# Seven stretches of zero matmuls on TensorE in the last quarter of a fused attention and rational-activation kernel

## Chip, cores and metric

The kernel runs on one core of a Trainium2 chip. The metric is the device time of one execution in microseconds (us), as the median of several runs. Beside it stands one profiled execution, whose trace gives the start, the duration and the reason for waiting of every instruction.

## What is computed

The reference is a polynomial-sketch linear attention followed by a two-layer network whose activation is a rational function. For 4 batches, 4 heads, 1088 positions and head size 32, with sketches S1 and S2 of rank 8:

```
phi(x)[i,j] = (S1 x)[i] * (S2 x)[j]            # 64 features per head
kv = sum_s phi(k) v^T ;  z = sum_s phi(k)
x  = (phi(q) kv) / (phi(q) z + 1e-6)           # 4352 tokens x 128
h  = x @ w_in                                  # 128 -> 2048
P  = a0 + a1 h + a2 h^2 + a3 h^3
Q  = 1 + |b0| |h| + |b1| h^2
out = (P / (Q + 1e-6)) @ w_out                 # 2048 -> 128
```

All inputs and the output are float32; the activation and the second layer are done in bfloat16.

## The kernel before

The tokens are split into chunks of 512 (the first into two of 256), and a last chunk of 256 gathers the 64 positions left over from each of the four batches. For each chunk the attention part makes `xT` (128 x tokens). The network part then goes through the 2048 hidden units in groups, numbered g0 to g22. A group of a full chunk is 8 blocks of 128 hidden units by 512 tokens, that is 4096 elements on each partition; the groups of the last chunk, g19 to g22, have 2048, 1024, 512 and 512. Each group takes these steps:

- TensorE multiplies `w_in` by `xT` into the PSUM buffer `h_ps` (line 793), and ScalarE copies it to `hb` in bfloat16 (line 799).
- VectorE makes |h|, the quadratic and the cubic by multiplications and scalings (lines 819 to 843 and 913 to 924); some sums are done by DMAs that add, issued by GpSimd (line 896).
- ScalarE makes 1/Q as exp(-ln Q): line 832 is the logarithm into `L`, line 836 the exponential into `u`.
- VectorE multiplies `y` by `u` (line 828).
- TensorE multiplies by the scaled `w_out` and adds up in the PSUM buffer `out_ps` (line 856, 8 matmuls of 512 columns for a full group; line 851 for the last chunk, by token). There are two forms: groups of terms "2" and "2d" have one such step with `u` and one with `y`, groups of terms "s" and "t" only the one with `y`. These steps are called "pr" (from u) and "py" (from y) here: py 16 is the one of g16.
- After the last group of a chunk ScalarE copies `out_ps` to `o_sb` (line 861), TensorE transposes that (line 866), ScalarE copies the transposes to `oT` (line 871) and SyncE stores it. The last chunk needs no transposes (line 981).

Buffers set much of the order: `out_ps` exists once, so the first product of the next chunk waits until ScalarE has copied it; `y` and `u` exist three times, so the first VectorE step that writes a new `y` (line 840 or 924) waits until the py step of three groups earlier has read its buffer. `kv_ps`, one PSUM bank, holds the key sums of a batch; the last batch's sums have been read before the stretches that matter here.

All steps are recorded with `plan.add(engine, ns, function, after=..., take=..., give=...)`, and `ORDER`, a fixed list of step numbers at the top of the file, says in which sequence they are issued. Each engine runs its own instructions strictly in that sequence. A new step takes the next free number and stands where `ORDER` names it.

The kernel already has matmuls whose result nobody reads: `warm` (line 352) multiplies a 128x128 by a 128x512 block of bfloat16 zeros, both read from one zero per partition. Eight of them stand at the very start and two in the first chunk, written to `out_ps`:

```python
def warm(n):
    for _ in range(n):
        nc.tensor.matmul(warm_ps[0], lhsT=zero.broadcast_to([128, 128]), rhs=zero.broadcast_to([128, CW]),
                         start=True, stop=True)
```

Of the kernel before, what the change touches and what calls it, by code (L numbers as in the profile page):

```python
# [12 lines left out]
FP = mybir.dt.float32  # L13
# [31 lines left out]
    566, 274, 275, 604, 603, 287, 277, 288, 622, 624, 627, 605, 610, 606, 586, 625, 567, 568, 626, 628, 642, 276,  # L45
    611, 523, 278, 644, 643, 612, 587, 607, 613, 289, 646, 279, 614, 645, 648, 635, 647, 280, 668, 290, 629, 569,
    649, 608, 669, 636, 637, 630, 670, 593, 291, 594, 631, 671, 638, 609, 651, 292, 293, 650, 652, 657, 653, 674,
    672, 294, 673, 689, 658, 659, 675, 615, 660, 616, 295, 632, 691, 676, 639, 431, 690, 692, 570, 693, 617, 682,
    571, 633, 695, 654, 634, 694, 661, 683, 618, 677, 684, 678, 572, 696, 717, 640, 655, 641, 698, 685, 656, 699,
    704, 697, 705, 715, 662, 716, 679, 706, 663, 718, 700, 686, 707, 732, 725, 746, 680, 687, 701, 664, 719, 726,  # L50
    733, 702, 681, 720, 703, 688, 619, 740, 760, 734, 741, 721, 727, 747, 735, 665, 722, 708, 736, 728, 723, 709,
    748, 710, 742, 749, 750, 711, 737, 743, 754, 729, 730, 755, 756, 724, 738, 666, 744, 731, 620, 739, 757, 761,
    667, 751, 762, 745, 768, 752, 763, 753, 712, 764, 769, 524, 765, 766, 525, 770, 713, 758, 759, 771, 714, 772,
    767, 773, 774, 775]


class Plan:
# [66 lines left out]
def kernel(  # L124
# [13 lines left out]
    nc = tc.nc  # L138
    B, H, S, D = q.shape
# [9 lines left out]
    CW = JC * 128  # L149
# [9 lines left out]
    WARM = (0, 0)  # L159
    GAPS = {}  # L160
    XWARM = (2, 0)
    ZEROS = 8
    USED = set(TERMS.values())
    ADDED = [i for i, kinds in ((1, "d1"), (0, "1")) if any(k in t for t in USED for k in kinds)]
# [15 lines left out]
    kvps = ctx.enter_context(tc.tile_pool(name="kvps", bufs=1, space=PSUM))  # L180
# [4 lines left out]
    plan = Plan(BUFS)  # L185
    T = {}

    def tile_of(pool, name, shape, dtype):
        return pool.tile(shape, dtype, name=name, bufs=BUFS[name])
# [110 lines left out]
    for b in range(2, B):  # L300
        for i, (name, go) in enumerate(mains(b)):
            ld[name, b] = load("SP", go, 1024 if name == "v" else 512, rank=-70 + i,
                               take=["v_aug" if name == "v" else "kq"])
# [3 lines left out]
    zero = nc.const_aps.tensor(0.0, (128, 1), FP).bitcast(BF)[:, 0:1]  # L307
# [42 lines left out]
# [5 lines that stand above are left out]
    def first_warm():  # L355
        warm_ps.append(ops.tile([128, CW], FP, name="out_ps", bufs=1))
        warm(ZEROS)

    c_zero = plan.add("DVE", 250, lambda: nc.vector.memset(zeros, 0.0), rank=-99)
    c_mask = plan.add("POOL", 1350, pool_mask, rank=-99.5)  # L360
    c_pool = plan.add("POOL", 1950, pool_consts, after=[c_mask], rank=-99)
    c_warm = plan.add("PE", 430 * ZEROS, first_warm, after=[], rank=-99, take=["out_ps"])

# [216 lines left out]
    def lab(n):  # L580
        return n - 1 if n > 1 else ("0", "0b")[n]

    def add_queries(n, nt, srcs, weights, kv_lhs, load_steps, kv_steps, w_steps, rank, give=(), early=False,
# [116 lines left out]
        def x_transposes(t):  # L700
            T["xTp", n, t] = tile_of(aps, "w_ps", [128, CW], FP)
            for i in range(2):
                nc.tensor.transpose(T["xTp", n, t][:, i * 128:(i + 1) * 128],
                                    in_=T["x", n][:, 2 * t + i].rearrange("p h d -> p (h d)"), identity=ident)
            warm(XWARM[n])

# [10 lines left out]
        def rest(s):  # L717
# [13 lines left out]
            else:  # L731
                dv = xe = xt = None
                nds = {}
                for t in range(nt // 2):
                    for hp in range(NP):
# [8 lines left out]
                                  take=["o_sb"] if t == 0 else [], give=["w_ps"], name=f"div {lab(n)},{t}")  # L744
                    s = plan.add("PE", 110 * 2 + 216 * XWARM[n], lambda t=t: x_transposes(t), after=[dv, xt], rank=rank + 0.05, take=["w_ps"],
                                 give=["o_sb"] if t == nt // 2 - 1 else [], name=f"x tr {lab(n)},{t}")
# [279 lines left out]
    for n in range(len(chunks) + 1):  # L1026

        rank = first_of[n] - 2.6
# [34 lines left out]
    for g, G in enumerate(groups):  # L1063
        G["x_step"] = x_steps[G["n"]]
        G["prev_o"] = o_step
        o_step = add_group(g, G)
    plan.issue()


# [28 lines left out]
```

## Time and profile before

| | |
|---|---|
| median of 3 runs | 266.84 us (266.09 to 266.88) |
| the profiled execution's own time | 266.53 us |
| its span, first to last instruction | 264.8 us, so 1.7 us lie around it |
| TensorE matmul | 236.0 us busy, 89% |
| VectorE | 243.2 us busy, 92% |
| ScalarE | 238.7 us busy, 90% |
| mean granted TensorE clock | 0.971 |

PE is TensorE's matmuls, PEld its weight loads, DVE VectorE, ACT ScalarE, POOL GpSimd. A number in square brackets on a line is the idle time of that engine just before it, with what ended it. PEclk is the share of TensorE's clock that was granted.

### The profile page before, as it was taken

What the parts mean: (1) busy time and instruction counts of PE and PEld (TensorE: products, weight loads), DVE (VectorE), ACT (ScalarE), POOL (GpSimd) and SP (SyncE); (2) the same over time, 40 slices, a digit from 0 to 9 for tenths busy, and PEclk for the clock granted to TensorE, in tenths of its full rate; (3) what the DMA queues carried; (4) which work ended last, traced back from release to release, by engine and by line L of the source; (5) the groups of instructions that cost most, each with busy time, mean ns of one, the idle gap of its engine ahead of it and who ended that gap; (6) DMA issues with size and microseconds to landing.
All of it is one profiled execution on the core that took longest, in us unless ns stands there. A gap on an engine that the chain in (4) does not pass through costs nothing.

```text
span 264.8 us, 3028 instructions
## 1 busy us (share of the span) xinstructions
PE 236.0 (89%) x1115; PEld 140.5 (53%) x1126; DVE 243.2 (92%) x240; ACT 238.7 (90%) x211; POOL 42.8 (16%) x63
## 2 busy tenths in 40 slices
PE   7999999999999999989899998999999788296561
PEld 4889897755656654434464545544434335153251
DVE  1658999989999999999999999999999999999882
ACT  3249798889989999999999999999999999999883
POOL 4800010101211112011201121101221111111000
PEclk9999999999999999999999999999999999769598
DMA  6987929953789996848798879954799978698512
GB/s 173 300 229 154 163 82 180 219 80 62 176 158 107 170 192 85 103 79 150 136 131 149 155 94 189 188 104 87 131 156 109 187 163 101 79 184 136 96 40 102
DMA packets 36607, 36.94 MB, mean 139 GB/s; under 512 B 18160, under 2 KB 30448, under 8 KB 36464
## 3 DMA queue, kind: packets, MB, share of 16 engines
q0 software_dynamic: 11664, 25.69, 62.2%
q1 hardware_dynamic: 24496, 10.95, 15.8%
q8 instruction: 9, 0.15, 0.2%
q10 hardware_dynamic: 432, 0.10, 0.2%
q14 instruction: 6, 0.05, 0.1%
HBM read 8.82 MB, written 2.23 MB: 42 GB/s over the span
## 4 chain that ended last, share of the span: by engine, by line
PE 44%; ACT 25%; DVE 21%; issue 8%; DVEq 0%; ACTq 0%
PE h_ps L793 20%; DVE y L828 9%; ACT L L832 7%; ACT hb L799 7%; ACT u L836 6%; PE out_ps L856 6%; PE kv_ps L488 6%; ACT u L808 3%; PE w_ps L452 2%; PE w_ps L606 2%; PE w_ps L653 2%; DVE u L828 2%; DVE y L840 2%; PE w_ps L666 2%; PE w_ps L442 2%
## 5 line engine op out<-in xcount | busy, mean ns | idle before, releaser
L793 PE MATMUL h_ps<-xT,w_in_sb 128*128 128x512 f32 (+1 forms) x320 | 126.6, 533 | 0.9 <-ACT hb L799 0.9
L793 PEld LDWEIGHTS h_ps<-xT,w_in_sb 128*128 128x128 f32 x320 | 57.6, 191 | 43.5 <-issue 34.5
L799 ACT CAST hb<-h_ps 128x1024 bf16<-128x1024 f32 (+1 forms) x70 | 70.8, 1036 | 5.7 <-PE h_ps L793 5.4
L836 ACT ACTIVATE u<-L 128x4096 bf16<-128x4096 f32 (+3 forms) x23 | 63.6, 2766 | 0.3
L828 DVE TENSOR_TENSOR y<-y,hb 128x4096 bf16<-128x4096 bf16 (+3 forms) x37 | 58.7, 1593 | 0.1
L832 ACT ACTIVATE L<-u,one_ap 128x4096 f32<-128x4096 bf16 (+3 forms) x17 | 43.4, 2553 | 0.5 <-DVE u L828 0.5
L828 DVE TENSOR_TENSOR y<-y,u 128x4096 bf16<-128x4096 bf16 (+3 forms) x23 | 39.8, 1729 | 0.2
L856 PEld LDWEIGHTS <-w_out 128*128 128x128 bf16 x208 | 20.9, 102 | 36.0 <-issue 21.8
L856 PE MATMUL out_ps<-y,w_out 128*128 128x512 bf16 (+1 forms) x136 | 33.4, 381 | 7.3 <-DVE y L828 6.8
L896 POOL DMA_DIRECT2D u<-lin x9 | 10.9, 1207 | 104.3 <-ACT ab L460 25.7
L832 ACT ACTIVATE L<-u,one_ap,b_rel 128x4096 f32<-128x4096 bf16 x6 | 23.2, 3872 | 0.0
L913 DVE TENSOR_TENSOR lin<-hb 128x4096 bf16<-128x4096 bf16 x9 | 20.6, 2286 | 0.0
L896 POOL DMA_DIRECT2D y<-lin x9 | 12.0, 1333 | 49.7 <-DVE y L828 15.7
L828 DVE TENSOR_TENSOR u<-lin,u 128x4096 bf16<-128x4096 bf16 (+3 forms) x14 | 19.2, 1373 | 0.2
L819 DVE TENSOR_SCALAR u<-hb 128x4096 int16<-128x4096 int16 (+3 forms) x20 | 18.5, 924 | 0.7 <-ACT hb L799 0.5
L896 POOL DMA_DIRECT2D y<-zeros x7 | 11.9, 1695 | 41.6 <-DVE y L828 23.2
L856 PE MATMUL out_ps<-u,w_out 128*128 128x512 bf16 (+1 forms) x62 | 13.6, 352 | 2.6 <-ACT u L836 2.4
L488 PEld LDWEIGHTS kv_ps<-v_aug,k_p 128*128 128x128 f32 x128 | 15.3, 192 | 1.1 <-DVE y L828 0.2
L488 PE MATMUL kv_ps<-v_aug,k_p 128*128 128x66 f32 x128 | 15.8, 273 | 0.0
L840 DVE TENSOR_SCALAR y<-hb,a_sb 128x4096 bf16<-128x4096 bf16 (+3 forms) x14 | 12.7, 910 | 1.5 <-PE out_ps L856 1.5
L660 ACT COPY q_pT<-w_ps 128x512 f32<-128x512 f32 (+1 forms) x20 | 10.5, 551 | 2.6 <-PE w_ps L653 2.6
L824 DVE TENSOR_SCALAR lin<-u,b_abs 128x4096 bf16<-128x4096 bf16 (+3 forms) x14 | 12.3, 877 | 0.0
(100 smaller groups left out, 255.6 us busy)
## 6 DMA issues: line engine op xcount, KB each, us to landing
u<-lin POOLq DMA_DIRECT2D x9, 1024.0 KB, 7.9
y<-lin POOLq DMA_DIRECT2D x9, 1024.0 KB, 8.3
y<-zeros POOLq DMA_DIRECT2D x6, 1024.0 KB, 11.0
out_dram<-oT SPq DMA_DIRECT2D x7, 256.0 KB, 3.7
kq<-in_k_dram SPq DMA_DIRECT2D x3, 512.0 KB, 5.3
v_aug<-in_v_dram SPq DMA_DIRECT2D x12, 128.0 KB, 5.3
kq<-in_q_dram SPq DMA_DIRECT2D x3, 512.0 KB, 4.3
w_in_sb<-in_moe_w_in_dram SPq DMA_DIRECT2D x1, 1024.0 KB, 5.4
```

What stands on the lines that cost most here:

```text
L488: nc.tensor.matmul(T["kv", b][:, hp * 66:(hp + 1) * 66], lhsT=lhs(hp), rhs=rhs(hp), start=(first and hp == 0), stop=final, skip_group_chec ...
L793: nc.tensor.matmul(T["h", g, s][:, i * W:(i + 1) * W], lhsT=w_in_sb[:, fi * 128:(fi + 1) * 128], rhs=T["xT", n][:, :W], start=True, stop=True)
L799: nc.scalar.copy(out=T["hb", g][:, s * W:(s + nsub) * W], in_=T["h", g, s][:, :nsub * W])
L819: nc.vector.tensor_scalar(out=u().bitcast(mybir.dt.int16), in0=hb().bitcast(mybir.dt.int16), scalar1=0x7FFF, scalar2=None, op0=AX.bitwise_and)
L824: nc.vector.tensor_scalar(out=lin(), in0=u(), scalar1=b_abs[:, 1:2], scalar2=b_abs[:, 0:1], op0=AX.mult, op1=AX.add)
L828: return lambda: nc.vector.tensor_mul(out=out(), in0=in0(), in1=in1())
L832: nc.scalar.activation(out=T["L", g, l0][:, :lw], in_=T["u", g][:, l0:l0 + lw], func=ACT.Ln, bias=one_ap, scale=b_rel[:, 0:1] if terms == ...
L836: nc.scalar.activation(out=T["u", g][:, l0:l0 + lw], in_=T["L", g, l0][:, :lw], func=ACT.Exp, scale=-1.0)
L840: nc.vector.tensor_scalar(out=y(), in0=hb(), scalar1=a_sb[:, 3:4], scalar2=a_sb[:, 2:3], op0=AX.mult, op1=AX.add)
L856: nc.tensor.matmul(T["o", n][:, :W], lhsT=W_terms[w][:, fis[i], :], rhs=T[src, g][:, i * W:(i + 1) * W], start=(start and i == 0), stop=(s ...
L896: nc.gpsimd.dma_start(out=dst(), in_=src(), accum_op=AX.add, max_dma_last_dim=4096)
L913: nc.vector.tensor_mul(out=sq(), in0=hb(), in1=hb())
```

## The change

Seven new steps on TensorE, numbered 776 to 782 and called hot 0 to hot 6, issue 2, 6, 23, 4, 18, 4 and 3 zero matmuls, 60 in all, of the same kind as `warm`. They write the `kv_ps` buffer, after the last batch's key sums were read from it, and nobody reads what they write. The order of all other steps stays, on TensorE and on every other engine. In TensorE's own sequence they stand here:

| step | zero matmuls | TensorE's instruction before it | and after it |
|---|---|---|---|
| hot 0 | 2 | h (L793) | the x products of the last chunk (L666, 64 columns) |
| hot 1 | 6 | h (L793) | pr 15 (L856 from u) |
| hot 2 | 23 | h (L793, 256 columns) | py 16 (L856 from y) |
| hot 3 | 4 | h (L793, 256 columns) | pr 17 (L856 from u) |
| hot 4 | 18 | h (L793, 256 columns) | the transposes of the chunk of g15 and g16 (L866) |
| hot 5 | 4 | these transposes | py 18 (L856 from y) |
| hot 6 | 3 | py 18 | pr 19 (L851 from u) |

Line numbers below the list HOT grow by one. The diff, with the lines of ORDER cut to the places where a number is new:

```diff
...
-    672, 294, 673, 689, ...
-    571, 633, 695, 654, 634, ...
...
+    672, 776, 294, 673, 689, ...
+    682, 571, 633, 695, 654, 777, 634, ...
+    ... 679, 706, 778, 663, 718, ...
+    ... 733, 702, 779, 681, 720, ... 747, 735, 780, 665, 722,
+    ... 723, 709, 748, 781, 710, 742, ... 755, 756, 782, 724, 738,
...
     XWARM = (2, 0)
+    HOT = [2, 6, 23, 4, 18, 4, 3]
     ZEROS = 8
...
         o_step = add_group(g, G)
+
+    hot_ps = []
+
+    def hot(n):
+        if not hot_ps:
+            hot_ps.append(tile_of(kvps, "kv_ps", [128, CW], FP))
+        for _ in range(n):
+            nc.tensor.matmul(hot_ps[0], lhsT=zero.broadcast_to([128, 128]), rhs=zero.broadcast_to([128, CW]),
+                             start=True, stop=True)
+
+    hs = None
+    for i, n in enumerate(HOT):
+        hs = plan.add("PE", 216 * n, lambda n=n: hot(n), after=[T["wr_step", B - 1], hs], rank=50, name=f"hot {i}",
+                      take=["kv_ps"] if hs is None else [])
     plan.issue()
```

## The prediction, made before the changed kernel ran

> **What bounds the kernel now.** I read the page first, for where TensorE's clock falls; then the chain of waits, for whether the end hangs on TensorE there; then TensorE's timeline and the windows, for how long each gap and each slow stretch is; and last the timelines of ScalarE and VectorE, for who waits. From the page, 40 slices of 6.6 us:
>
> ```profile
> PE   7999999999999999989899998999999788296561
> DVE  1658999989999999999999999999999999999882
> ACT  3249798889989999999999999999999999999883
> PEclk9999999999999999999999999999999999769598
> ```
>
> VectorE and ScalarE are full nearly to the end, and TensorE has gaps only in the last six slices, where its clock falls twice. So a slow TensorE costs nothing unless one of the other two is left without work. The chain shows the one place where that happens:
>
> ```profile
> 248.61 0.59 PE out_ps L856
> ...
> 249.41 2.78 PE out_ps L856 x6
> ...
> 252.22 0.42 DVE y L840
> ```
>
> That is py 18. Ahead of it the chain runs on VectorE, behind it on VectorE and ScalarE. TensorE's timeline (start, length, number; idle time before in brackets):
>
> ```profile
> 219.26 1.89 PE L856 MATMUL out_ps<-u,w_out 128*128 128x512 bf16 x8 [1.72 <-ACT u L836]
> ...
> 232.34 3.55 PE L856 MATMUL out_ps<-y,w_out 128*128 128x512 bf16 x8 [5.58 <-DVE y L828]
> ...
> 246.56 1.11 PE L866 MATMUL w_ps<-ident,o_sb 128*128 128x128 f32 x4 [3.77 <-ACT oT L871]
> ...
> 249.41 2.77 PE L856 MATMUL out_ps<-y,w_out 128*128 128x512 bf16 x6 [0.22 <-issue]
> ```
>
> The same eight matmuls take 1.89 us after a gap of 1.72, but 3.55 after one of 5.58; py 18 (one of its eight records is missing) runs from 248.61 to 252.19, 3.58 us. The windows, cut where the clock changes (length, busy time by engine, granted clock, DMA share, GB/s):
>
> ```profile
> 225.54:228.95 3.41, 1.22 (x6) 0.84 (x5) 3.41 (x4) 3.41 (x2) 0.00 (x0) 0.99 0.86 99
> 228.95:232.36 3.41, 0.02 (x1) 0.02 (x1) 3.41 (x3) 3.41 (x2) 1.17 (x1) 0.50 0.43 77
> ...
> 242.60:246.01 3.41, 0.20 (x1) 0.00 (x0) 3.38 (x6) 3.41 (x2) 0.59 (x1) 0.99 0.75 86
> 246.01:249.43 3.42, 1.71 (x6) 1.11 (x8) 3.31 (x5) 3.39 (x5) 0.00 (x0) 0.50 0.80 145
> 249.43:252.84 3.41, 2.75 (x6) 0.87 (x6) 1.89 (x5) 2.04 (x3) 0.00 (x0) 0.51 0.00 0
> 252.84:256.25 3.41, 2.15 (x36) 1.98 (x36) 3.27 (x5) 3.38 (x5) 0.00 (x0) 1.00 0.03 5
> ```
>
> The clock drops near 228.95 and 246.0 and returns near 235.7 and 252.8; all four lie on one grid of 3.41 us. It dropped after stretches in which TensorE was busy 1.22 us or less, returned after stretches of 3.42 and 2.75, did not return after 1.71, and held after 2.15. Last, who waits:
>
> ```profile
> 237.19 0.58 ACT L861 COPY o_sb<-out_ps 128x512 f32<-128x512 f32 x1
> ...
> 248.93 1.91 ACT L836 ACTIVATE u<-L 128x2048 bf16<-128x2048 f32 x1
> 252.22 0.58 ACT L861 COPY o_sb<-out_ps 128x512 f32<-128x512 f32 x1 [1.38 <-PE out_ps L856]
> ...
> 250.05 0.68 DVE L828 TENSOR_TENSOR y<-y,hb 128x1024 bf16<-128x1024 bf16 x1
> 252.22 0.41 DVE L840 TENSOR_SCALAR y<-hb,a_sb 128x512 bf16<-128x512 bf16 x1 [1.49 <-PE out_ps L856]
> ```
>
> ScalarE waits 1.38 us for `out_ps` and VectorE 1.49 us for the `y` buffer that py 18 reads. The copy at 237.19, which takes the slow py 16's result, waits for nothing: that slow stretch is free.
>
> **What the change adds.** Sixty zero matmuls, each with its weight load. One costs 0.22 us at full clock: the second warm matmul of the first chunk starts at 17.39 and the transposes behind it at 17.61; the eight of 1.89 us above give (1.89 - 0.38) / 7 = 0.216. That is 13.0 us on TensorE, and what matters is whether each stretch ends before the instruction behind it could start.
>
> - hot 0: 2 x 0.216 = 0.43 in a gap of 0.82 (before the x products at 206.92). Free. hot 1: 1.30 in 1.72. Free.
> - hot 2: 23 x 0.216 = 4.97, from 226.76 to 231.73; py 16 waits for `y` until 232.34. Free. The clock is then full at 232.34, and py 16 ends at 234.23 instead of 235.89. Its cover is 0.61 us.
> - hot 3: no gap in the trace of before, where TensorE is busy from 235.71 to 242.80. But py 16 now ends 1.66 earlier and the h products behind it (2.6 us of issue) by about 236.8, while pr 17 waits for ScalarE's exponential, which ends at 237.30. Four zeros take 0.86 and end at 237.7, before the 238.31 at which pr 17 started. Free.
> - hot 4: 18 x 0.216 = 3.89. With pr 17 some 0.6 earlier TensorE arrives at 242.2 rather than 242.80, so they end by 246.1, and the transposes wait for ScalarE until 246.56. If it arrives only at 242.80 they end at 246.69, 0.13 late; that is hidden too, since at full clock the transposes end 0.5 earlier (0.60 for 1.11) and py 18 can't start before VectorE is done at 248.56.
> - hot 5: 0.86 behind the transposes, to 248.0 or 248.2; py 18 starts at 248.61. hot 6: 0.65 behind py 18, to 251.15; pr 19 waits for ScalarE's copy until about 251.4. Free with 0.25 to spare.
>
> **What it removes.** No stretch of TensorE's idle time above 0.7 us is left from 226.8 to 250.5, so the clock holds, if zeros count as work for it. The start of the trace says that they do: TensorE does nothing but eight zero matmuls there, their weight loads stand 0.43 us apart until 3.36, and the next one follows after 0.36:
>
> ```profile
> 3.36 0.15 PEld L352 LDWEIGHTS <-const-float32-0.0 128*128 128x128 bf16 x1 [0.28 <-issue]
> 3.72 0.57 PEld L442 LDWEIGHTS w_ps<-ident,kq 128*128 128x128 f32 x4 [0.21 <-issue]
> ```
>
> The transposes behind then take 1.21 us for eight, 0.13 apart, nearer to the warm 0.11 than to the slow 0.21. So at 248.61 py 18 starts at full clock and ends at 248.61 + 1.89 = 250.50 instead of 252.19. What is late next is the two engines' own work: ScalarE's exponential ends at 250.84, so its copy starts 1.38 earlier; VectorE's multiplication ends at 250.73, so line 840 starts 1.49 earlier. 0.34 and 0.23 us of the 1.69 that TensorE saves are thus lost. From 252.22 to 258.07 VectorE does not wait; its inputs from ScalarE come early by 0.7 us (the exponential that ended at 254.94 is used at 255.73; `hb` of 255.90 at 256.67); and ScalarE's own idle 0.50 at 258.16 is a wait for VectorE. So the end moves by VectorE's 1.49, or by 1.38 if a ScalarE result is late after all. I take 1.45.
>
> Nothing hangs on the extra writes: the PSUM bank is `kv_ps`'s own, and ScalarE's exponentials of 4096 took 3.62 to 3.64 us and VectorE's multiplications 2.28 to 2.29 whether TensorE was busy or idle, so I put contention at nothing, with 0.1 us either way. The sum is 266.53 - 1.45 = 265.1 on the profiled execution, which lay 0.31 under the median of the runs; on the median it is 265.4. I say 265.2.
>
> **Rivals.** *Fillers longer than the gaps (slower).* If a weight load can't hide behind the matmul before it, a zero matmul takes 0.216 + 0.102 (line 856's mean weight load) = 0.318. hot 2 then ends at 234.07 and from there TensorE never waits: py 16 1.73, h 2.6, hot 3 1.27, pr 17 and py 17 3.46, h 0.86, hot 4 5.72, transposes 0.44, hot 5 1.27, so py 18 starts at 251.43 and ends at 253.32, 1.13 later than before: 267.7. In the same sum py 18 starts at 235.85 + 49 times the price of one filler, so the gain is whole up to 0.26 us and gone at 0.295. The rows of 0.216 and 0.22 are each with a weight load per matmul, and speak against it. [...] Chance 0.05.
>
> *Zeros do not hold the clock.* Then the clock falls inside hot 4 or before; at 0.427 each hot 4 and 5 take 7.7 and 1.7 us, the transposes 1.1, and py 18 goes from 253.3 to 256.9, 4.7 later at worst: 269 to 271. The loads at the start speak against it. Chance 0.03.
>
> *The grid lies elsewhere.* Shift it, and the second slow stretch of before can begin late in py 18 or end within it: py 18 would end between 250.6 and 252.2, so the loss that the change can remove is anywhere from 0.1 to 1.5. The spread of the runs, 266.09 to 266.88, would fit that. Shifted, a drop could also fall into the tail, where TensorE has gaps above 1 us; its last products of 0.4 us would each take 0.2 more, up to 0.5 together. This gives 265.4 to 266.6. [...] Against: the profiled execution had the whole loss and was not slower than the median. Chance 0.14, of which 0.06 is still faster by more than the bound.
>
> **Numbers.** About 0.3%, 0.8 us, is what a measurement of this kernel can tell from no change. The forecast has 0.78. Faster: 0.78 + 0.06 = 0.84; within the bound 0.08; slower 0.05 + 0.03 = 0.08. The range: the sum with all of 1.49, less 0.3 for the spread of the runs, is 264.7; above, it takes in the shifted grid, 266.6. Outside lie the two slower rivals and a little more.
>
> **What would show it.** Right: a granted clock of 1.00 from 226 to 260; py 16 and py 18 at about 1.89 us; hot 4 ending before 246.7; the copy to `o_sb` near 250.8 without a wait above 0.1, line 840 near 250.75; all behind as before, 1.4 to 1.5 earlier. Wrong: zero matmuls above 0.26 us apart, py 18 starting after 248.7, a granted clock below 1 in the gaps, or a new wait on ScalarE or VectorE between 226 and 250.

## The result, and the profile after

The changed kernel takes 265.04 us (median of 7 runs, 264.58 to 265.56) against 266.70 for the kernel before in the same rounds (266.04 to 266.90): a ratio of 0.994, 95% interval 0.9925 to 0.9956. It is faster by about 1.7 us, and the forecast was 265.2. The profiled execution took 264.85 us with a span of 263.1 (before 266.53 and 264.8), at a mean granted clock of 0.996.

The page of the changed kernel, in its 40 slices:

```profile
PE   8999999999999999989899998999999899999971
DVE  1658999979999999999999999999999999999992
ACT  3249798889989999999999999999999999999993
PEclk9999999999999999999999999999999999999998
```

The two dips of the clock are gone; the windows show 1.00 until 261 us, when all computing is over. TensorE's timeline through both gaps, with the zeros in line 1075:

```profile
226.68 5.19 PE L1075 MATMUL kv_ps<-const-float32-0.0 128*128 128x512 bf16 x23
232.42 1.89 PE L857 MATMUL out_ps<-y,w_out 128*128 128x512 bf16 x8 [0.54 <-DVE y L829]
234.14 2.75 PE L794 MATMUL h_ps<-xT,w_in_sb 128*128 128x256 f32 x12
...
242.35 4.10 PE L1075 MATMUL kv_ps<-const-float32-0.0 128*128 128x512 bf16 x18
246.66 0.66 PE L867 MATMUL w_ps<-ident,o_sb 128*128 128x128 f32 x4 [0.21 <-ACT oT L872]
247.15 1.03 PE L1075 MATMUL kv_ps<-const-float32-0.0 128*128 128x512 bf16 x4
248.51 1.89 PE L857 MATMUL out_ps<-y,w_out 128*128 128x512 bf16 x8 [0.32 <-DVE y L829]
250.23 0.81 PE L1075 MATMUL kv_ps<-const-float32-0.0 128*128 128x512 bf16 x3
251.46 1.05 PE L852 MATMUL out_ps<-w_out,u 128*128 128x128 bf16 x16 [0.42 <-ACT o_sb L862]
```

Each stretch of zeros shown here ends before what stands behind it is ready: the wait in brackets is still for VectorE or ScalarE. py 16 and py 18 take 1.89 us. The two instructions that waited for py 18, on ScalarE and on VectorE, now wait for nothing:

```profile
250.85 0.56 ACT L862 COPY o_sb<-out_ps 128x512 f32<-128x512 f32 x1
```

```profile
250.55 0.41 DVE L841 TENSOR_SCALAR y<-hb,a_sb 128x512 bf16<-128x512 bf16 x1
```

VectorE's instruction stood at 252.22 before, and the last copy moves from 260.49 to 258.82: 1.67 us at both places.

### The profile page after: what moved, and what is told of

Its sections match the earlier page's. It is cut to its first block, busy times and chain, and to the rows that moved or that the text cites. A ratio compares the mean times of both kernels' runs of the same rounds, so it can differ in the third digit from the quotient of the medians.

```text
span 263.1 us, 3159 instructions
## 1 busy us (share of the span) xinstructions
PE 246.8 (94%) x1186; PEld 145.6 (55%) x1186; DVE 242.8 (92%) x240; ACT 238.6 (91%) x211; POOL 43.0 (16%) x63
## 5 line engine op out<-in xcount | busy, mean ns | idle before, releaser
L857 PEld LDWEIGHTS <-w_out 128*128 128x128 bf16 x208 | 20.2, 98 | 27.6 <-issue 11.8
L857 PE MATMUL out_ps<-y,w_out 128*128 128x512 bf16 (+1 forms) x144 | 30.8, 355 | 1.1 <-DVE y L829 1.1
L1075 PE MATMUL kv_ps<-const-float32-0.0 128*128 128x512 bf16 x60 | 14.2, 381 | 0.0
```

Source lines behind the costliest of these rows:

```text
L857: nc.tensor.matmul(T["o", n][:, :W], lhsT=W_terms[w][:, fis[i], :], rhs=T[src, g][:, i * W:(i + 1) * W], start=(start and i == 0), stop=(s ...
L1075: nc.tensor.matmul(hot_ps[0], lhsT=zero.broadcast_to([128, 128]), rhs=zero.broadcast_to([128, CW]), start=True, stop=True)
```

## The experiments

Two theories stood against each other. *py 18 only*, the prediction's: the first gap's slow stretch is hidden, and the second gap earns it all. *Both gaps*: the slow stretch behind the first gap costs something too. All kernels below are the changed one with another list HOT. Each table row compares with runs of the kernel before that were made beside it; those ranged from 266.04 to 268.24, more than the three runs at the start had shown.

| kernel | us, median (range) | ratio to before, 95% interval | before beside it |
|---|---|---|---|
| e1: second gap alone | 265.29 (264.61 to 266.10) | 0.9938 (0.9913 to 0.9962) | 267.03 |
| e2: first gap alone | 266.22 (265.91 to 266.87) | 0.9968 (0.9952 to 0.9984) | 267.03 |
| e3: 8 zeros in the second gap | 266.75 (264.61 to 267.66) | 0.9973 (0.9945 to 1.0001) | 267.03 |
| e4: 34 zeros in the second gap | 267.44 (266.86 to 267.80) | 1.0010 (0.9995 to 1.0025) | 267.03 |
| e5: the change once more | 264.97 (264.40 to 265.24) | 0.9907 (0.9882 to 0.9932) | 267.47 |
| e6: without hot 0, 1 and 3 | 264.66 (264.41 to 265.25) | 0.9902 (0.9877 to 0.9926) | 267.47 |
| e7: without hot 2 and 4 | 267.00 (266.09 to 267.87) | 0.9984 (0.9964 to 1.0004) | 267.47 |
| e8: two more, in the tail | 264.93 (264.66 to 264.97) | 0.9907 (0.9880 to 0.9933) | 267.47 |

**e1, the second gap alone.**

```diff
-    HOT = [2, 6, 23, 4, 18, 4, 3]
+    HOT = [0, 0, 0, 0, 18, 4, 0]
```

> Only hot 4 (18 zeros) and hot 5 (4) are left; hot 0 to 3 and hot 6 issue nothing. If the whole gain comes from py 18 running at full clock, and the slow py 16 is hidden behind ScalarE's exponential, the time is that of the changed kernel, 265.0 to 265.3 us, with py 16 still at about 3.55 us in the trace and py 18 at 1.89. If the first gap's zeros earn part of the gain, it is 265.6 to 266.7.

The time is as *py 18 only* has it, 0.25 us above the changed kernel's, with ranges that overlap. But the trace shows two things that this theory did not have. TensorE and VectorE:

```profile
232.11 3.57 PE L857 MATMUL out_ps<-y,w_out 128*128 128x512 bf16 x8 [5.58 <-DVE y L829]
235.48 3.26 PE L794 MATMUL h_ps<-xT,w_in_sb 128*128 128x256 f32 x12
...
253.62 1.89 PE L852 MATMUL out_ps<-w_out,y 128*128 128x128 bf16 x16 [0.97 <-DVE y L829]
```

```profile
242.30 0.55 DVE L841 TENSOR_SCALAR y<-hb,a_sb 128x1024 bf16<-128x1024 bf16 x1 [0.44 <-PE out_ps L857]
```

The clock came back at 236.5, 0.8 us later than in the profiled execution of before, so the h products took 3.26 instead of 2.77; py 17 came later, and VectorE waited 0.44 us for the `y` buffer that py 17 reads (line 841, the first to write the `y` of g20). And the clock fell once more, to 0.50 at 253.6, in the tail, where this kernel has no hot 6: py 19 took 1.89 instead of 1.07.

**e2, the first gap alone.**

```diff
-    HOT = [2, 6, 23, 4, 18, 4, 3]
+    HOT = [0, 0, 23, 0, 0, 0, 0]
```

> Only hot 2 (23 zeros in the first long gap). If py 16 is hidden, the time is that of the kernel before, 266.5 to 266.9 us: py 16 takes 1.89 us, but the clock still falls in the second gap and py 18 takes 3.4 to 3.6. If the first gap matters, it is 265.9 us or less. If the gain came from VectorE's two instructions at 242 us, which took 0.90 and 0.57 us before and 0.54 and 0.42 after, and not from the clock, this kernel has the gain or not by that alone.

It is faster than before by 0.3%, interval 0.2 to 0.5%: *py 18 only* falls, though the time, 266.22, lies above the 265.9 that was put for the other. py 18 was slow in it (3.21 us), and VectorE waited 1.12 us for it:

```profile
248.55 3.21 PE L857 MATMUL out_ps<-y,w_out 128*128 128x512 bf16 x8 [1.20 <-DVE y L829]
...
251.79 0.41 DVE L841 TENSOR_SCALAR y<-hb,a_sb 128x512 bf16<-128x512 bf16 x1 [1.12 <-PE out_ps L857]
```

e1 and e2 save 1.74 and 0.81 us against the same runs of before, 2.55 together. The whole change saves 2.50 in e5, but beside other runs of before, whose median lay 0.44 higher; that the two savings add up is not shown. The third theory named there, VectorE's two quicker instructions, falls too: this execution has them (0.54 and 0.42 us) and still ends 1.5 us of span later than the changed kernel's.

**e3, fewer zeros.**

```diff
-    HOT = [2, 6, 23, 4, 18, 4, 3]
+    HOT = [0, 0, 0, 0, 8, 4, 0]
```

> Hot 4 with 8 zeros instead of 18, hot 5 with 4, the others nothing: 1.73 us of zeros in the second gap and some 2.0 us left idle. The trace of before shows a drop after 2.19 us idle in a window of 3.41 and none after 1.26, so this lies between. If the clock holds with that much idle, the time is 265.0 to 265.3 us; if it drops, py 18 is slow for most of its length and the time 266.0 to 266.7. If the clock fell only after a whole idle window of 3.41 us, it would hold here in any case.

Neither of the two: of 12 runs five lie between 264.61 and 265.55, seven between 266.73 and 267.66, none between. The profiled execution was one of the five (265.24 us); its clock stayed at 1.00 through 2.01 us of idle time:

```profile
242.93 1.91 PE L1075 MATMUL kv_ps<-const-float32-0.0 128*128 128x512 bf16 x8
246.85 0.66 PE L867 MATMUL w_ps<-ident,o_sb 128*128 128x128 f32 x4 [2.01 <-ACT oT L872]
```

The same program with the same gap either pays about 1.7 us (266.94 against 265.26, the medians of the two groups) or does not. The seven were not profiled, but the mean granted clock of every run was recorded: 0.981 in each of the five, 0.974 or 0.975 in each of the seven. So the clock was lower in the seven. The difference, 0.006 to 0.007 of 265 us, is about what one stretch of 3.41 us at a clock of 0.50, like the one in e2's trace from 247.8 to 251.3, takes off (1.7 us); where in the run it lay was not recorded, and the first gap, unfilled here, adds its own spread.

**e4, too many zeros.**

```diff
-    HOT = [2, 6, 23, 4, 18, 4, 3]
+    HOT = [2, 6, 23, 4, 34, 4, 3]
```

> Hot 4 with 34 zeros instead of 18, the rest as changed. 16 more at 0.216 us are 3.46 us: hot 4 ends near 249.7 instead of 246.24, the transposes follow, then hot 5, and py 18 starts near 251.1 instead of 248.51 and ends near 253.0, 2.6 us late. If TensorE sets the end there, the time is 267.6 us, slower than the kernel before by 0.9 in spite of the full clock. If TensorE had slack behind py 18, it stays near 265.

The time came out as expected, 2.4 us above the changed kernel. With the clock at 1.00 until 262.8, when the last matmul is over, py 18 starts at 251.55, and both engines wait for it longer than they did for the slow one in any trace here (ScalarE 2.08):

```profile
253.48 0.41 DVE L841 TENSOR_SCALAR y<-hb,a_sb 128x512 bf16<-128x512 bf16 x1 [2.39 <-PE out_ps L857]
```

So TensorE does set the end there. The distance to before, +0.4 us, is less than the 0.9 expected mainly because before was at 267.03 in these rounds, not 266.7.

**e5, e6 and e7: which stretches count.**

> The changed kernel itself once more, beside the three that follow and the same runs of before, because only hot 2, without the second gap, had already given a ratio of 0.997 to before, where the prediction called the first gap free. If both gaps earn, this is the fastest of these: about 0.994, 265.0 us, against 0.997 for the first gap alone and 0.994 or a little above for the second alone. The trace should show the clock at 1.00 through both gaps.

```diff
-    HOT = [2, 6, 23, 4, 18, 4, 3]
+    HOT = [0, 0, 23, 0, 18, 4, 3]     # e6
+    HOT = [2, 6, 0, 4, 0, 4, 3]       # e7
```

> Without hot 0, hot 1 and hot 3, the rest as changed: 48 zeros instead of 60. If only the two gaps of 5.6 and 3.8 us bring the clock down, this is the same as the changed kernel within 0.2 us (265.0), and the clock in the trace stays at 1.00 from 200 to 252 us. If the gaps of 0.8 to 1.7 us matter too, together with their neighbours, a drop shows in the trace and the time is 265.3 to 266.0.

> The counterpart: hot 2 and hot 4 issue nothing, the five small stretches stay (19 zeros). The clock falls in both long gaps as before, and the time is that of the kernel before, 266.5 to 267.0 us, if the two long stretches are the whole of it. If the small ones earn part of the gain, the time lies between.

e5 came out as expected, at 264.97, with the clock at 1.00 through both gaps. e6 is at least as good (264.66, ranges overlapping), and its clock is 1.00 from 200 to 259 us: hot 0, 1 and 3 bring nothing that these runs show. e7 without the two long stretches is before again, within its interval. Its profiled execution, of 267.69 us, happened to be one of its longer ones, and it shows what the profile of before did not. TensorE, ScalarE, and VectorE:

```profile
232.78 3.57 PE L857 MATMUL out_ps<-y,w_out 128*128 128x512 bf16 x8 [5.57 <-DVE y L829]
236.14 4.01 PE L794 MATMUL h_ps<-xT,w_in_sb 128*128 128x256 f32 x12
```

```profile
239.32 1.01 ACT L800 CAST hb<-h_ps 128x1024 bf16<-128x1024 f32 x1 [1.11 <-PE h_ps L794]
```

```profile
244.59 0.55 DVE L841 TENSOR_SCALAR y<-hb,a_sb 128x1024 bf16<-128x1024 bf16 x1 [2.06 <-PE out_ps L857]
253.38 0.41 DVE L841 TENSOR_SCALAR y<-hb,a_sb 128x512 bf16<-128x512 bf16 x1 [0.61 <-PE out_ps L857]
```

Here the slow stretch lay from 231.8 to 238.7 and not from 228.9 to 235.7 as in before, with py 16 only 0.44 us later. The h products behind py 16 took 4.01 us instead of 2.77, ScalarE waited 1.11 for them and VectorE 2.06 for py 17. The second slow stretch ended within py 18 (2.70 us instead of 3.58), so VectorE's wait there was only 0.61. So the two prices change places as the drops of the clock move; together they were 1.5 us of VectorE's waiting in the trace of before and 2.7 in that of e7.

**e8, two stretches more, in the tail.**

```diff
-    HOT = [2, 6, 23, 4, 18, 4, 3]
+    HOT = [2, 6, 23, 4, 18, 4, 3, 4, 3]   # 783 in ORDER after 724, 784 before 759
```

> The changed kernel with two stretches more: 4 zeros between pr 19 and py 19 (a gap of 0.96 us) and 3 between the last transposes and py 21 (0.81). In the traces of the kernels with only one gap filled the clock fell at 253.7 or 254.7 us for some 3 us, in the tail, where py 19 then took 1.89 instead of 1.07. If that happens in some executions of the changed kernel too, this one is 0.1 to 0.3 us faster, 264.8, and less spread; if not, it is the same, 265.0. If the zeros come in the way of py 19 or py 21 it is slower by up to 0.3.

The median is that of the change (264.93 and 264.97). The range of its six runs is 0.31 us against 0.84 for e5, too few runs to call it steadier. Neither profile of the changed kernel has a drop in the tail.

## Why the prediction was right, and where it was not

**Cost of the zeros: right.** All 60 took 378 to 383 ns each, and 23 took 5.19 us, so they follow each other every (5.19 - 0.38) / 22 = 0.219 us, where 0.216 was put, with a weight load for each. py 16 waited 0.54 for `y` (0.61 put), the transposes 0.21, pr 19 0.42 (0.25 put). The rival with fillers longer than the gaps is out: it needs 0.318 us for load and matmul together, and the trace has 0.219. That an overrun moves the end by about as much as it delays py 18, as that rival's working has it, is shown by e4 (2.4 and 2.6 us).

**Zeros hold the clock: right.** 1.00 through both gaps in the changed kernel, e5, e6 and e8, against 0.50 behind each of them in before. The rival is out.

**py 18 and what is late next: right in mechanism, 0.2 short.** py 18 ended at 250.40 (250.50 put) and ScalarE's copy stood at 250.85, where the end of its own exponential had put it. VectorE's line 841 was at 250.55 instead of 250.73, since VectorE itself was earlier. Lines 841 and 820 of g20 (840 and 819 in before) had taken 0.90 and 0.57 us in before and took 0.54 and 0.42 here, and GpSimd's DMA issue beside them 1.75 instead of 1.29:

```profile
241.90 1.29 POOL L896 DMA_DIRECT2D y<-zeros  x1 [5.68 <-DVE y L828]
```

```profile
241.99 1.75 POOL L897 DMA_DIRECT2D y<-zeros  x1 [5.69 <-PE out_ps L857]
```

VectorE then waited 0.28 for ScalarE, so about 0.1 to 0.2 of that half microsecond is left. The prediction had no term for this, and it goes with the first gap's zeros: all six traces of kernels with hot 2 have 0.54 or 0.55, 0.42 and 1.75, and none of the four without has all three. Why is open. The sum was 1.45, the span moved 1.7.

One reading was a little off: by the profile's page TensorE has gaps not only in the last six slices but also in the three before (7, 8 and 8), where hot 0 and hot 1 went. e6 does without them and loses nothing.

**"That slow stretch is free": wrong, and the medians hide it.** The statement held in the profiled execution of before, but it rested on ScalarE's copy at 237.19 alone. The other instruction that hangs on that stretch is VectorE's line 840 of g20, at 242.04 behind py 17, which ended at 241.93; the prediction left it out:

```profile
240.04 1.89 PE L856 MATMUL out_ps<-y,w_out 128*128 128x512 bf16 x8
```

```profile
242.04 0.90 DVE L840 TENSOR_SCALAR y<-hb,a_sb 128x1024 bf16<-128x1024 bf16 x1
```

The cover was 0.1 us at most, and perhaps none: in e1, e3 and e7, where VectorE did wait here, it also began 0.11 us behind the end of py 17. In those traces the clock came back later than at 235.7 (236.5 in e1 and e3, 238.7 in e7), and the cover was gone: 0.44 us of waiting in e1, 0.47 in e3, 2.06 in e7. In runs, filling the first gap alone is worth 0.8 us (e2). That the forecast gain of 1.45 came out beside the first rounds (1.66) was in part luck: the profiled execution of before had its first slow stretch where it costs nothing, and none of those rounds' runs of before was as long as many of the later ones were. Beside e5's runs of before the same change gained 2.50.

**The grid lies elsewhere: right that it moves, wrong in what that was said to do.** Its place differs from execution to execution: the first drop is near 228.95 in before, 229.7 in e1 and e3, 231.8 in e7, while py 16 started within 0.7 us of the same time in all four. The prediction had this as something that makes the change worth less, because only the second stretch was priced. It can also make the kernel before slower, by the first stretch; before ranged over 2.2 us in the 47 runs beside the experiments. Their mean granted clocks sort them: 21 have 0.967 or 0.968, and these took 267.32 to 268.24 us; the other 26 have 0.970 to 0.976 and took 266.04 to 267.30. The first rounds had none of the long ones (266.90 at most), those beside e1 to e4 10 in 30, those beside e5 to e8 11 in 17. With them the worth of the change goes from 1.66 us beside the first rounds to 2.50 beside the last, while its own time moved by 0.07. None of the 12 runs of e2, where the first gap is filled, reached 267. No long run of before was profiled, so which stretch makes it long is argued from e2 and e7; why their share changed (other rounds, another chip for the last) is open.

**What stays open.** Even the kernels whose profiled clock never fell before the end range over 0.3 to 1.0 us. VectorE's and GpSimd's half microsecond is no part of it, since they all have it alike. In the profiles of four of them (the change, e5, e6 and e8; e4 has its overrun) the spread is made at the start, where matmuls run slowly at first: in the changed kernel's first profile the weight loads of the zero matmuls of `warm` stand 0.43 us apart from 1.23 to 3.37 us, against 0.219 for the zeros of hot 2, though the granted clock reads 1.00 there. The eight transposes behind them, in two executions of the same program, the changed kernel's first profile and e5:

```profile
4.22 1.43 PE L443 MATMUL w_ps<-ident,kq 128*128 128x128 f32 x8
```

```profile
4.21 1.91 PE L443 MATMUL w_ps<-ident,kq 128*128 128x128 f32 x8
```

By their pace the slow part lasted longer in e5, and the clock's grid lies later there too: the drop after all computing stands at 262.7 instead of 261.1 (mean granted clock 0.998 against 0.996). The next transpose (of `k_rem`) starts at 7.72, 8.12, 7.56 and 7.84 us in the four, and from there to the end of the span all four take 255.3 to 255.5. That the pace at the start makes the difference is seen in these two; for e6 and e8, and for runs without a profile, it is not shown. That a low clock sets this pace is the author's estimate: at a clock of 0.50 the weight loads of py 16 in before stood 0.43 us apart too.

What decides whether the clock falls was not shown; the traces give single cases. In before it fell after a stretch of 3.41 us with 2.19 us idle. In e3 steps of 3.41 us lead from the drop at 229.7 to the one at 253.6; in the step from 243.4 to 246.8 TensorE was busy for 1.46 us and the clock stayed at 1.00, in the one from 250.2 to 253.6 it was busy for 1.43 and the clock fell to 0.50. In e2 a step with 1.56 us busy (from 241.0) was followed by 1.00 and another with 1.56 (from 251.2) by 0.50. So these stretches, with 1.43 to 1.56 us busy, went either way, and busy time alone does not tell which.

## What to carry to other kernels

Where one engine waits for several microseconds and its clock falls (here 5.58 and 3.77 us, and to 0.50), look for the first instruction on the path that it serves afterwards, and fill the gap with work that ends before that instruction is ready: here two long stretches that together cost nothing bring 0.6 to 1.0%, and one that overran by 2.6 us gave it all back. Before calling a slow stretch hidden, list every engine that waits for its results and how much time each has to spare; one with 0.1 us to spare is not hidden but lucky. When the cause has another place in another execution, as the first drop here (228.9 to 231.8 us), one profile shows one of these places: compare runs made side by side, take the widest of several traces, and sort the runs without a trace by their mean granted clock.

## What the runs showed of the hardware

In the trace of before the two drops and the two returns of the clock lie on steps of 3.41 us (228.95, 235.8, 246.0 and 252.8). Where these steps lie, counted from the first instruction, differs between executions: the same first gap brought the first drop at 228.9, 229.7 and 231.8 us in four traces. What sets their place was not shown. A gap of about 2 us may or may not come with a lower clock (e3: 2.01 us idle at 1.00 in the profiled execution, and two groups of runs 1.2 us apart with nothing between, at mean granted clocks of 0.981 and 0.974 to 0.975).

In every trace where GpSimd's issue of a DMA ran at the same time as VectorE's lines 841 and 820 of g20 (840 and 819 in before), one of the two took longer, or both, and which of them differs between the kernels. In e7, where the issue is over before VectorE begins, neither does: 0.55 and 0.42 us, and 1.29. In before VectorE took 0.90 and 0.57 beside 1.29, that is 0.51 more than with hot 2, where it took 0.54 and 0.42 beside 1.75, that is 0.46 more for GpSimd. In e1 both lost a little (0.56 for 0.42, and 1.39 for 1.29). Why was not shown.
